# Talking-heads attention with a squared-ReLU FFN: the last 64 keys of two chunks post-mixed together

## The chip, the cores and the metric

The kernel runs on one core of a Trainium2 chip. The metric is the device time of one execution in microseconds (us). Before the change it was 520.69 us, the median of three runs (520.1 to 522.92).

## The reference

Eight batches of 12-head attention, 448 queries and keys, head size 64, in which the heads are mixed twice: the scores by `w_pre` ahead of the softmax, the probabilities by `w_post` behind it. A two-layer FFN with a squared ReLU follows.

```python
scores = scale * np.matmul(q, k.transpose(0, 1, 3, 2))           # (8, 12, 448, 448)
scores = np.einsum('bhij,hg->bgij', scores, w_pre)
attn = np.exp(scores - np.max(scores, axis=-1, keepdims=True))
attn = attn / (np.sum(attn, axis=-1, keepdims=True) + 1e-09)
attn = np.einsum('bhij,hg->bgij', attn, w_post)
x = np.matmul(attn, v)                          # to (8 * 448, 12 * 64) rows
h = np.maximum(x @ w_in, 0.0)                   # w_in (768, 2048)
return (h * h) @ w_out                          # w_out (2048, 768)
```

## The kernel before

Every engine's instructions are written out by a planner. `ORDER` is a string of digits, each naming a stream of TensorE units (0 transposes of q and k, 1 QK, 2 pre-mix, 3 post-mix, 4 attention times v, 5 direct chunks of batch 0, 6 and 7 the first FFN layer, 8 and 9 the second); TensorE runs the units in this order. The other engines' work is placed by the planner when its inputs are due, by the costs in the code; a copy out of PSUM marked `FLEX` goes to ScalarE (ACT) or VectorE (DVE). GpSimd (POOL) folds and issues the loads and most stores in one queue, SyncE (SP) issues the moves from `stage` to `dring`.

*Attention.* A unit of QK gives 128 (or 64) queries of a head pair; its scores go through `stage`, and a DMA brings them to `dring`, where a chunk of 10 queries has its 12 heads on the partitions. The pre-mix is a matmul over these 120 rows. ACT takes the exponential into the ring `pring` (12 chunks) and sums each row (`rowsum`). DVE takes the reciprocal (`rinv`), and POOL (DVE for the first chunks) folds it into the post-mix weights: `wk2s` = `wk2b` x `rinv`, for a pair of chunks at a time.

*Post-mix* (`emit_post`). The exponentials are the stationary operand, 128 keys at a time, `wk2s` (60 columns) the moving one. A chunk's two halves of 5 queries stand on partitions 0 to 59 and 64 to 123, and run as two row tiles side by side. 448 keys are three and a half slots of 128: there are four slots (`NS`, `KEYS`), and two of them share 64 keys, so that a pair of chunks takes 16 matmuls. The result goes by two evictions of 480 columns to `a2t`, keys on partitions, one `a2t` for each half of a batch (220 and 228 queries).

*Attention times v* (`emit_AV`), once for each half batch, a "part". `vraw` holds the keys of v in the same four slots. In a part, 40 matmuls over 128 keys stand in 128x64 tiles (heads on two column tiles), and 8 matmuls over 64 keys in 64x64 tiles (`fn_half`, ahead of the others) serve the slots that are used by half; for the last heads a zeroed half of `vraw` is multiplied along. Three evictions, one for each pair of head pairs, bring the result to `xt`, the FFN's input.

*FFN.* From batch 2 on it runs in row tiles or 64x64 tiles, in two phases, so that a second phase waits for the first. Tile shapes on TensorE in the order's rows: QK with 128 rows, post-mix, L1278 and L1413 are row tiles; pre-mix, transposes, L1292 and L1427 are 64x64; L1211 is 128x64; L1257 and L1362 use the whole array.

## Time and profile before

| | |
|---|---|
| median of 3 runs | 520.69 us |
| the profiled execution: its span | 520.6 us |
| TensorE busy | 505.5 us (97%), 10859 matmuls |
| ACT busy | 425.6 us (82%) |
| DVE busy | 398.7 us (77%) |
| POOL busy | 203.4 us (39%) |
| TensorE's clock | full in all 40 slices |

The span reaches from the first to the last instruction of the profiled execution, which is all of its own time that the page has. Busy shares are means over stages: the kernel starts with direct matmuls for batch 0 and ends with the FFN of batch 7 alone. In the profile a line number is that of the program; most copies have the one line of a helper (L526 on ACT, L527 on DVE), so the tile's name tells them apart. PEld is the load of a stationary operand, which overlaps the matmuls.

### The profile page before, as it was taken

The page shows a single profiled execution, that of the slowest core. Times are in us where ns is not written, and L with a number is a line of the kernel's source. Part 1 is how long each engine was busy: PE and PEld are TensorE (multiplying, and loading weights), DVE is VectorE, ACT ScalarE, POOL GpSimd, SP SyncE. Part 2 cuts the span into 40 slices and gives each one's busy share as a digit, 9 for nine tenths or more (in the row PEclk, how much of TensorE's full clock was granted, in tenths as well). Part 3 has the DMA queues.
Part 4 walks back from the last instruction along what each step waited for, and adds up shares of the span by engine and source line. Part 5 has one row for each costly group of instructions (what it writes and reads, how often), then busy time and mean ns, then how long its engine had stood idle before and what let it go on. Part 6 is the DMA issues. An engine that isn't in the chain of part 4 may idle for free.

```text
span 520.6 us, 25670 instructions
## 1 busy us (share of the span) xinstructions
PE 505.5 (97%) x10859; PEld 340.1 (65%) x10859; DVE 398.7 (77%) x1004; ACT 425.6 (82%) x1206; POOL 203.4 (39%) x404
## 2 busy tenths in 40 slices
PE   8999999899999999999999999999999999999996
PEld 4555777668766665667657665667666666678963
DVE  6967988789987869967997779976887669757430
ACT  4799999879998898989887999988788879878311
POOL 9914364325632384134622464225440333123010
PEclk9999999999999999999999999999999999999999
DMA  8999999646893699347974689457972568432013
GB/s 160 208 218 184 197 194 184 156 107 144 167 180 86 136 177 197 92 112 166 178 156 90 153 175 179 98 111 170 167 151 59 125 140 148 91 81 69 4 39 90
DMA packets 82724, 72.12 MB, mean 139 GB/s; under 512 B 13578, under 2 KB 80090, under 8 KB 82602
## 3 DMA queue, kind: packets, MB, share of 16 engines
q0 software_dynamic: 36944, 32.81, 38.5%
q1 hardware_dynamic: 45370, 37.38, 29.7%
q8 instruction: 89, 1.46, 1.1%
q14 instruction: 33, 0.27, 0.1%
q10 hardware_dynamic: 288, 0.20, 0.1%
HBM read 45.70 MB, written 11.01 MB: 109 GB/s over the span
## 4 chain that ended last, share of the span: by engine, by line
PE 92%; DMA 3%; DVE 2%; issue 2%; ACT 1%; POOL 0%; DVEq 0%
PE ps L1413 17%; PE ps L1278 12%; PE ps L1427 9%; PE ps L1292 9%; PE ps L1133 8%; PE ps L1052 8%; PE ps L1257 6%; PE ps L1211 6%; PE ps L922 5%; PE ps L974 4%; DMA dring<-stage 3%; PE ps L825 2%; PE ps L1362 2%; PE ps L986 2%; PE ps L649 1%
## 5 line engine op out<-in xcount | busy, mean ns | idle before, releaser
L1070 ACT ACTIVATE pring<-ps 128x448 bf16<-128x448 f32 x360 | 192.0, 550 | 12.6 <-PE ps L1052 7.3
L1101 POOL TENSOR_TENSOR wk2s<-wk2b,rinv 128x120 bf16<-128x120 bf16 (+1 forms) x179 | 69.0, 389 | 223.5 <-DVE rinv L1094 222.8
L527 DVE CAST a2t<-ps 128x480 bf16<-128x480 f32 (+1 forms) x201 | 122.1, 640 | 18.4 <-PE ps L1133 16.9
L527 DVE CAST stage<-ps 128x448 bf16<-128x448 f32 (+1 forms) x189 | 112.8, 618 | 19.0 <-PE ps L986 8.7
L526 ACT ACTIVATE stage<-ps 128x448 bf16<-128x448 f32 (+1 forms) x171 | 87.9, 549 | 18.2 <-PE ps L986 10.6
L526 ACT ACTIVATE a2t<-ps 128x480 bf16<-128x480 f32 x167 | 88.2, 570 | 15.5 <-PE ps L1133 15.0
L1413 PE MATMUL ps<-w_out_sb,h2t 64*128 64x384 bf16 x1056 | 95.9, 322 | 0.0
L1070 ACT ACTIVATION_READ_ACCUMULATOR pring<-ps 128x1 f32 x360 | 76.9, 214 | 0.0
L1133 PEld LDWEIGHTS ps<-wk2s,pring 60*128 60x128 bf16 x2880 | 54.9, 93 | 24.7 <-issue 5.8
L1278 PE MATMUL ps<-xt,w_in_sb 64*128 64x448 bf16 (+2 forms) x840 | 70.6, 309 | 0.0
L1413 PEld LDWEIGHTS ps<-w_out_sb,h2t 64*128 64x128 bf16 x1056 | 48.4, 94 | 31.1 <-PE ps L1052 0.7
L1459 POOL DMA_DIRECT2D out_dram<-osb x59 | 36.9, 632 | 75.9 <-DVE osb L527 25.8
L1133 PE MATMUL ps<-wk2s,pring 60*128 60x60 bf16 x2880 | 62.3, 187 | 1.9 <-issue 1.4
L1052 PE MATMUL ps<-dring,wk 64*64 64x448 bf16 (+1 forms) x676 | 61.5, 359 | 2.4 <-issue 1.2
L1427 PE MATMUL ps<-w_out_sb,h2t 64*64 64x384 bf16 x1216 | 57.4, 323 | 0.9 <-issue 0.8
L1323 DVE TENSOR_SCALAR h1t<-ps 128x448 bf16<-128x448 f32 (+2 forms) x96 | 46.2, 488 | 12.6 <-PE ps L1278 9.1
L1292 PE MATMUL ps<-xt,w_in_sb 64*64 64x448 bf16 (+1 forms) x1008 | 54.5, 345 | 0.8 <-issue 0.6
L1332 DVE TENSOR_TENSOR h2t<-h1t 128x448 bf16<-128x448 bf16 (+2 forms) x176 | 52.0, 331 | 1.4 <-ACT h1t L1322 0.9
L1322 ACT ACTIVATE h1t<-ps 128x448 bf16<-128x448 f32 (+2 forms) x80 | 35.4, 448 | 19.7 <-PE ps L1278 13.9
L1094 DVE RECIPROCAL rinv<-rowsum 128x2 f32<-128x2 f32 (+1 forms) x184 | 29.3, 160 | 28.2 <-ACT pring L1070 27.1
L1278 PEld LDWEIGHTS ps<-xt,w_in_sb 64*128 64x128 bf16 x840 | 38.3, 94 | 18.1 <-DVE rinv L1094 0.5
L1427 PEld LDWEIGHTS ps<-w_out_sb,h2t 64*64 64x64 bf16 x1216 | 38.2, 107 | 13.8 <-issue 2.0
(70 smaller groups left out, 595.0 us busy)
## 6 DMA issues: line engine op xcount, KB each, us to landing
dring<-stage SPq DMA_DIRECT2D x309, 105.0 KB
out_dram<-osb POOLq DMA_DIRECT2D x45, 192.0 KB, 3.7
qraw<-in_q_dram POOLq DMA_DIRECT2D x42, 112.0 KB, 5.3
kraw<-in_k_dram POOLq DMA_DIRECT2D x42, 112.0 KB, 6.2
w_in_sb<-in_moe_w_in_dram POOLq DMA_DIRECT2D x8, 384.0 KB, 16.3
w_out_sb<-in_moe_w_out_dram POOLq DMA_DIRECT2D x8, 384.0 KB, 11.9
vraw<-in_v_dram POOLq DMA_DIRECT2D x21, 128.0 KB, 4.8
vraw<-in_v_dram POOLq DMA_DIRECT2D x21, 96.0 KB, 5.0
```

The lines of the kernel that those rows point to most:

```text
L526: return eng.activation(o, i_, AF.Copy)
L527: return eng.tensor_copy(o, i_)
L1052: r_ = eng.matmul(ps[64 * y:64 * y + 64, gr.banks[x], 0:S], wk1[64 * x:64 * x + 64 - R0 * x, :], dring[64 * x:64 * x + 64 - R0 * x, (g0 + ...
L1070: return eng.activation(pring[:, pr, 0:S], ps[:, gr.banks[x], 0:S], AF.Exp, accum_out=rowsum[:, rs, :])
L1101: return eng.tensor_tensor(wk2s[:, p0:p0 + n, :], i0.to_broadcast([128, n, PR]), rinv[:, p0:p0 + n, :].to_broadcast([128, n, PR]), ALU.mult)
L1133: r_ = eng.matmul(ps[:, gr.banks[x], o0:o0 + PR], pring[64 * x:64 * x + PR, pr + y, j0:j0 + 2 * PJ], wk2s[64 * x:64 * x + PR, pr + y, :], ...
L1278: r_ = eng.matmul(ps[:, g.banks[x], 0:n], w_in_sb[64 * y:64 * y + 64, ft, t * 128:(t + 1) * 128], xt[64 * y:64 * y + 64, ft, c0:c1], start ...
L1292: r_ = eng.matmul(ps[64 * z:64 * z + 64, g.banks[x], 0:n], w_in_sb[64 * y:64 * y + 64, ft, t:t + 64], xt[64 * y:64 * y + 64, ft, c0:c1], s ...
L1323: return eng.tensor_scalar(h1t[:, box[0], 0:n], ps[:, g.banks[x], 0:n], 0.0, None, op0=ALU.max)
L1332: return eng.tensor_tensor(h2t[:, t16, o0:o0 + n], h1t[:, box[0], 0:n], h1t[:, box[0], 0:n], ALU.mult)
L1413: r_ = eng.matmul(ps[:, g.banks[hh], 0:FH], h2t[64 * y:64 * y + 64, t16, col:col + 128], w_out_sb[64 * y:64 * y + 64, t16, hh * FH:(hh + 1 ...
L1427: r_ = eng.matmul(ps[64 * z:64 * z + 64, g.banks[hh], 0:FH], h2t[64 * y:64 * y + 64, t16, col + 64 * z:col + 64 * z + 64], w_out_sb[64 * y ...
```

## The change

The keys are cut into three whole slots of 128 and a rest of 64 (`NS` = 3, `NM` = 7 blocks of `a2t` in place of 8).

*Fold.* `pring` gets 60 more columns behind the 448 exponentials, with a copy of `wk2b` (`wk2c`, once, on ACT), and the fold multiplies the last 128 columns of each chunk (64 exponentials and the 60 weights with 4 zeros) by `rinv`: 256 elements for a pair, not 120.

*Post-mix.* The three whole slots go as before, 12 matmuls for a pair. The rest of both chunks goes in one matmul on each row tile: the scaled exponentials of both are the stationary operand (64 + 64 columns), the unscaled `wk2b` the moving one. The first chunk's rest then stands on partitions 0 to 63, the second's on 64 to 127. A pair takes 14 matmuls and two evictions of 420 columns; the single last chunk of a batch takes 8, as before.

*Attention times v.* 36 matmuls over 128 keys come first, 12 for each of three banks. The rest follows in three phases of 8 matmuls in 64x64 tiles (`avq..._0` to `_2`), each with 110 or 118 columns. Each waits for the phase before it, and the banks are complete after the second phase (one) and the third (two). `a2t` now holds one member's queries of each pair behind the other's, so each `xt` eviction is two copies of 220 columns with a permuted target, and a third one of 16 columns in a second half.

*Loads, constants, order.* `vraw` has six slots, all loads of v bring four of them (128 KB), and q and k of batches 2 to 7 may load ten chunks earlier. The planner's constants and the string `ORDER` are new.

```diff
-MODE_SWITCH = 106.0
+MODE_SWITCH = 100.0
-FETCH = (2450.0, 0.3, 2400.0, 0.3, 600.0)
+FETCH = (3560.0, 0.3, 2400.0, 0.3, 600.0)
 ORDER = (
-    "0001501510105151555555555555555551335510015555555553335510021551355553255310055511255321"
...
+    "0010150011055115555555555555515555555550033551115555501105553335352555535131500555211555"
...
-    NS = 4
-    POS = (0, 3, 5, 1, 4, 6, 2)
-    KEYS = (0, 3 * PJ, 5 * PJ, PJ)
+    NS = 3
+    NM = 2 * NS + 1
+    POS = (0, 2, 4, 6, 1, 3, 5)
+    KT = NS * 2 * PJ
...
+        def fn_wk2c(eng, en):
+            i_ = wk2b[:, :, :].rearrange("p a b -> p (a b)").unsqueeze(1).to_broadcast(
+                [128, NPS, PR])
+            return eng.activation(pring[:, :, S:S + PR], i_, AF.Copy)
...
-            s0, n = (0, NS) if (h0 == 4) == (u == 1) else (u, NS - 1)
+            n = NS + 1
...
-                            after = [chain["t"], pre_at((b - 1) * NCP + 2 + 2 * n)]
+                            after = [chain["t"], pre_at((b - 1) * NCP - 8 + 2 * n)]
...
             def fn_fold(eng, en):
-                i0 = wk2b[:, :, :].rearrange("p a b -> p (a b)").unsqueeze(1)
                 return eng.tensor_tensor(
-                    wk2s[:, p0:p0 + n, :], i0.to_broadcast([128, n, PR]),
-                    rinv[:, p0:p0 + n, :].to_broadcast([128, n, PR]), ALU.mult)
+                    wk2s[:, p0 // 2, :, 0:n, :].rearrange("p k y e -> p y k e"),
+                    pring[:, p0:p0 + n, KT:].rearrange("p y (k e) -> p y k e", k=2),
+                    rinv[:, p0:p0 + n, :].unsqueeze(2).to_broadcast([128, n, 2, PJ]), ALU.mult)
...
                 for y in range(n):
                     for s in range(NS):
-                        o0 = (y * NS + s) * PR
+                        o0 = (n * s + y) * PR
                         for x in range(2):
                             r_ = eng.matmul(
                                 ps[:, gr.banks[x], o0:o0 + PR],
-                                pring[64 * x:64 * x + PR, pr + y, j0:j0 + 2 * PJ],
-                                wk2s[64 * x:64 * x + PR, pr + y, :],
+                                pring[64 * x:64 * x + PR, pr + y, 2 * PJ * s:2 * PJ * (s + 1)],
+                                wk2s[64 * x:64 * x + PR, pr // 2, 1, y, 0:PR],
                                 start=True, stop=True,
                             )
+                o0 = n * NS * PR
+                for x in range(2):
+                    r_ = eng.matmul(
+                        ps[:, gr.banks[x], o0:o0 + PR],
+                        wk2s[64 * x:64 * x + PR, pr // 2, 0, :, :].rearrange("p y e -> p (y e)"),
+                        wk2b[64 * x:64 * x + PR, :, :].rearrange("p a b -> p (a b)"),
+                        start=True, stop=True,
+                    )
...
+            done_at = ((), (1,), (0, 2))
...
+            for ph in range(NP // 2):
+                use = (ph, (ph + 1) % (NP // 2))
+
+                def fn_rest(eng, en, ph=ph, use=use):
+                    r_ = None
+                    for x in range(2):
+                        for z, kk in QUADS:
+                            bank = use[z]
+                            h = 2 * (2 * bank + x) + kk
+                            o0 = (2 * x + z) * al
+                            w = AL[0] if z else al
+                            r_ = eng.matmul(
+                                ps[kk * 64:kk * 64 + 64, gs[bank].banks[0], o0:o0 + w],
+                                vraw[64 * z:64 * z + 64, h, 0 if z else NS + 1, :],
+                                a2t[half][64 * z:64 * z + 64, h, 2 * NS, 0:w],
+                                start=False, stop=(x == 1 and bank in done_at[ph]),
+                            )
+                    return r_
+
+                was = t_av
+                t_av = unit(s_AV, "avq%d_%d_%d" % (b, c0, ph), fn_rest, [was],
+                            2 * (al / 2.4 + 6.0), "quad", None, 8)
+                t_av.sync = [was]
...
                 def fn_x(eng, en, p=p, g=g):
...
+                    for a in range(2):
+                        d = xt[:, p + a, c0:c0 + n].rearrange(
+                            "p (m c t) -> p m c t", c=2, t=CH // x_)
+                        r_ = copy(eng, en, d, src[:, a, :, 0:AL[0]].rearrange(
+                            "p c (m t) -> p m c t", t=CH // x_))
+                    if al > AL[0]:
+                        r_ = copy(eng, en, xt[:, p:p + 2, c0 + n:c1], src[:, :, 0, AL[0]:al])
```

Where the order moves TensorE, two places. The rows are TensorE's instructions in order: line, result and operands, shape of the result, how many alike. First, the attention times v of the first half of batch 6 before the change (L825 transposes, L1292 first FFN layer, L974 QK, L1052 pre-mix, L1427 second FFN layer):

```order
L1292 MATMUL ps<-xt,w_in_sb 64x448 x24
L1190 MATMUL ps<-a2t0,vraw 64x220 x8
L974 MATMUL ps<-qkt 64x448 x4
L1211 MATMUL ps<-a2t0,vraw 64x220 x40
L1052 MATMUL ps<-dring,wk1 64x448 x8
L1427 MATMUL ps<-w_out_sb,h2t 64x384 x32
```

and after it (L836 transposes, L985 QK, L1063 pre-mix, L1469 second FFN layer, L1209 and L1235 attention times v):

```order
L985 MATMUL ps<-qkt 64x448 x4
L1209 MATMUL ps<-a2t0,vraw 64x220 x36
L1235 MATMUL ps<-a2t0,vraw 64x110 x8
L1063 MATMUL ps<-dring,wk1 64x448 x4
L1235 MATMUL ps<-a2t0,vraw 64x110 x8
L1469 MATMUL ps<-w_out_sb,h2t 64x384 x32
L1235 MATMUL ps<-a2t0,vraw 64x110 x8
```

The 64x64 matmuls moved from ahead of the 128x64 ones to behind them, in three pieces with another unit between two of them. Elsewhere a post-mix unit, in row tiles, stands between.

Second, the way from the second half of batch 3 to the first FFN layer, before (L1133 post-mix):

```order
L1211 MATMUL ps<-a2t1,vraw 64x228 x40
L974 MATMUL ps<-qkt 128x448 x2
L1133 MATMUL ps<-wk2s,pring 128x60 x16
L1052 MATMUL ps<-dring,wk1 64x448 x4
L1292 MATMUL ps<-xt,w_in_sb 64x448 x24
```

and after, from the end of the third phase (L1320 first FFN layer, L1144 and L1152 post-mix):

```order
L1235 MATMUL ps<-a2t1,vraw 64x118
L1235 MATMUL ps<-a2t1,vraw 64x110
L1063 MATMUL ps<-dring,wk1 64x448 x4
L985 MATMUL ps<-qkt 128x448 x2
L1320 MATMUL ps<-xt,w_in_sb 128x448 x12
L1144 MATMUL ps<-wk2s,pring 128x60 x12
L1152 MATMUL ps<-wk2b,wk2s 128x60 x2
```

Between the last matmul over v and the first of the FFN stood three units, now two; post-mix units follow behind.

More of the change, by code (lines that the diff above doesn't have):

```diff
@@ L462, in bass_talking_heads_attention__then__ffn_squared_relu_kernel @@
         wall = early[:, 512:512 + NP * 2 * H].rearrange("p (n x h) -> p n x h", n=NP, x=2)
-        pring = sb("pring", [128, NPS, S], DT.bfloat16)
-        a2t = [sb("a2t%d" % i, [128, NS, H, HC[i] * CH], DT.bfloat16) for i in range(2)]
+        pring = sb("pring", [128, NPS, 512], DT.bfloat16)
+        AL = (HC[0] * H5, HC[0] * H5 + TAIL)
+        a2t = [sb("a2t%d" % i, [128, H, NM, AL[i]], DT.bfloat16) for i in range(2)]
         xt = sb("xt", [128, NP, S], DT.bfloat16)
@@ L1224, in fn_x @@
-                def fn_x(eng, en, p=p, g=g, x_=x_):
-                    return copy(eng, en, xt[:, p:p + 2, c0:c1],
-                                ps[:, g.banks[x_], 0:2 * n].rearrange("p (x n) -> p x n", x=2))
+                                    ps[kk * 64:kk * 64 + 64, g.banks[0],
+                                       2 * x * al:2 * (x + 1) * al],
+                                    vraw[:, h, s + 1, :],
+                                    a2t[half][:, h, 2 * s:2 * s + 2, :],
+                                    start=(x == 0 and s == 0), stop=False,
+                                )
@@ new lines, in fn_av @@
+                    return r_
+                avs.append(unit(s_AV, "av%d_%d_%d" % (b, c0, p), fn_av,
+                                a2 + v_of[b] + ([t_zero[0]] if half else []),
+                                2 * NS * (2 * al / 2.4 + 2.9), "cols", g, 4 * NS))
+            t_av = None
+            done = {}
+            for ph in range(NP // 2):
[19 more added lines that the diff above has]
+                t_av.sync = [was]
+                t_av.after += [avs[i] for i in use]
+                for i in done_at[ph]:
+                    done[i] = t_av
@@ new lines, in emit_AV, with fn_x @@
+            for p in range(0, NP, 2):
+                g = gs[p // 2]
+                def fn_x(eng, en, p=p, g=g):
+                    n = 2 * AL[0]
+                    x_ = 1 if b * NCP + c0 < ND else 2
+                    src = ps[:, g.banks[0], 0:4 * al].rearrange(
+                        "p (a c n) -> p a c n", a=2, c=2)
+                    for a in range(2):
[5 more added lines that the diff above has]
+                        r_ = copy(eng, en, xt[:, p:p + 2, c0 + n:c1], src[:, :, 0, AL[0]:al])
+                    return r_
+                more = 200.0 if half else 70.0
@@ L1486, in bass_talking_heads_attention__then__ffn_squared_relu_kernel @@
                 t_wk2 = add("wk2", DVE, fn_wk2, [t_wsmall, t_mask2], {DVE: (300.0, 400.0)}, -450.0)
+                t_wk2c = add("wk2c", ACT, fn_wk2c, [t_wk2], {ACT: (820.0, 930.0)}, -2e6)
                 emit_load_qk(1)
```

130 lines of the change are left out of this document (54 added, 76 removed).

## The prediction

> **What bounds the kernel now.** I read the page first, then the busy time by stage, then TensorE's timeline at an attention-times-v part, then groups by shape and the waits. The page gives the shares and the chain that ended last:
>
> ```profile
> span 520.6 us, 25670 instructions
> PE 505.5 (97%) x10859; PEld 340.1 (65%) x10859; DVE 398.7 (77%) x1004; ACT 425.6 (82%) x1206; POOL 203.4 (39%) x404
> PE 92%; DMA 3%; DVE 2%; issue 2%; ACT 1%; POOL 0%; DVEq 0%
> ```
>
> TensorE carries 92% of the chain; ACT and DVE have a fifth to spare, GpSimd (POOL) more than half. The busy times by stage say where TensorE still stands still:
>
> ```profile
> 48.00:100.00 52.00, 48.14 (x1010) 36.30 (x1010) 44.64 (x127) 47.70 (x141) 23.08 (x47) 1.00 0.99 187
> 100.00:200.00 100.00, 98.49 (x2178) 69.69 (x2180) 83.84 (x212) 90.30 (x265) 46.27 (x93) 1.00 0.72 145
> 484.00:521.00 37.00, 31.57 (x428) 22.93 (x416) 8.88 (x32) 7.85 (x18) 2.52 (x4) 0.98 0.18 47
> ```
>
> From 48 to 100 us it lacks 3.9 us, from 100 to 200 us 1.5 us, and the last stage lacks 5.4 us, most of it behind the last matmul (last evictions and output). The profiled execution's span is 520.6 us, 0.1 us under the median of the runs (520.69), so I sum against 520.6.
>
> A saturated stretch of TensorE's timeline gives its prices (start, length, work, count; a unit's price is start to start, as matmuls overlap):
>
> ```profile
> 250.90 0.39 PE L1133 MATMUL ps<-wk2s,pring 60*128 60x60 bf16 x16
> 251.12 0.35 PE L974 MATMUL ps<-qkt 64*128 64x448 bf16 x2
> ...
> 253.81 0.54 PE L974 MATMUL ps<-qkt 64*128 64x448 bf16 x4
> 254.28 0.38 PE L1052 MATMUL ps<-dring,wk 64*64 64x448 bf16 x4
> 254.49 1.31 PE L1292 MATMUL ps<-xt,w_in_sb 64*64 64x448 bf16 x24
> 255.63 0.36 PE L1052 MATMUL ps<-dring,wk 64*64 64x448 bf16 x4
> 255.82 1.31 PE L1292 MATMUL ps<-xt,w_in_sb 64*64 64x448 bf16 x24
> ```
>
> A post-mix unit of 16 matmuls takes 0.22 us, 13.75 ns each. Four 64x448 matmuls in 64x64 tiles take 0.19 us, and 24 take 1.14 us (254.49 to 255.63): 47.5 ns each, 0.106 ns a column. A change of tile shape has a price of its own: the four row-tiled QK matmuls at 253.81 need 2 x 0.19 = 0.38 us, but the next unit, in 64x64 tiles, starts 0.47 us later. So 0.09 us, and 0.1 us with the other direction in mind.
>
> **The change, part by part.**
>
> *Post-mix.* A pair of chunks takes 14 matmuls for 16; the single last chunk of a batch keeps 8. 8 batches x 22 pairs x 2 x 13.75 ns = 4.8 us less on TensorE, all on the path.
>
> *Attention times v.* One part's matmuls and the way to the next layer, before:
>
> ```profile
> 243.54 2.16 PE L1211 MATMUL ps<-a2t,vraw 128*64 128x228 bf16 x40
> 245.63 0.36 PE L974 MATMUL ps<-qkt 64*128 64x448 bf16 x2
> 245.83 0.39 PE L1133 MATMUL ps<-wk2s,pring 60*128 60x60 bf16 x16
> 246.15 0.38 PE L1052 MATMUL ps<-dring,wk 64*64 64x448 bf16 x4
> 246.36 1.31 PE L1292 MATMUL ps<-xt,w_in_sb 64*64 64x448 bf16 x24
> ```
>
> 40 matmuls of 228 columns take 2.09 us with one change of shape behind them: 1.99 us, 0.218 ns a column. A second half had 40 x 228 of these and 8 x 228 in 64x64 tiles (1.99 + 0.19 = 2.18 us); it gets 36 x 236 and 12 x (118 + 110) (1.85 + 0.29 = 2.14). A first half goes from 40 x 220 and 8 x 220 (1.92 + 0.19 = 2.11) to 36 x 220 and 24 x 110 (1.73 + 0.28 = 2.01). Over eight of each 0.14 x 8 = 1.1 us; small matmuls never run quite at the rate of wide ones, so I take 0.9 us. Work on TensorE: -5.7 us.
>
> *Changes of tile shape.* The rest's three 64x64 phases must not run into each other, so each waits for the one ahead, and the order puts other units between. Counted over TensorE's whole order, the shape changes 224 times before and 255 times now. 31 x 0.1 = +3.1 us, all on the path. Here more than half of the saved work is given back.
>
> *Waits of TensorE on itself.* 32 new ones (second and third phase of 16 parts). In 29 a unit stands between, in 3 (batch 0) nothing. The nearest rows are a second phase of the first FFN layer behind one short unit:
>
> ```profile
> 258.93 1.46 PE L1292 MATMUL ps<-xt,w_in_sb 64*64 64x448 bf16 x24
> 260.07 0.51 PE L974 MATMUL ps<-qkt 64*64 64x448 bf16 x4
> 260.45 0.76 PE L1292 MATMUL ps<-xt,w_in_sb 64*64 64x448 bf16 x12
> ```
>
> Here the second phase starts 0.38 us behind the short unit, not 0.19: a wait of 0.19 us, with 448 columns draining. That is the upper end for a covered wait of 110 columns, 29 x 0.19 = 5.5 us; the lower end is nothing, as where a post-mix or pre-mix unit covers it elsewhere. The bare ones cost at most 0.39 us, the length of a post-mix unit's drain (250.90). I take 3 x 0.2 + 29 x 0.01 = +0.9 us, since 110 columns drain sooner than 448.
>
> *Evictions.* An `a2t` eviction falls from 480 to 420 columns; the groups by shape price a column:
>
> ```profile
> L527 DVE CAST a2t<-ps 128x480 bf16<-128x480 f32 x193 | 119.6, 651 | 16.6 <-PE ps L1133 15.2
> L526 ACT ACTIVATE a2t<-ps 128x480 bf16<-128x480 f32 x159 | 86.1, 582 | 13.4 <-PE ps L1133 12.8
> L527 DVE CAST a2t<-ps 128x192 bf16<-128x192 f32 x8 | 2.8, 354 | 1.7 <-PE ps L1133 1.7
> L526 ACT ACTIVATE a2t<-ps 128x192 bf16<-128x192 f32 x8 | 2.7, 339 | 2.1 <-PE ps L1133 2.1
> L1101 POOL TENSOR_TENSOR wk2s<-wk2b,rinv 128x120 bf16<-128x120 bf16 x171 | 66.8, 393 | 219.9 <-DVE rinv L1094 219.2
> L1101 POOL TENSOR_TENSOR wk2s<-wk2b,rinv 128x60 bf16<-128x60 bf16 x8 | 2.3, 290 | 3.7 <-DVE rinv L1094 3.6
> L1322 ACT ACTIVATE h1t<-ps 128x220 bf16<-128x220 f32 x22 | 7.7, 364 | 3.0 <-PE ps L1278 2.1 <-PE ps L1292 0.5
> L526 ACT ACTIVATE xt<-ps 128x456 bf16<-128x456 f32 x13 | 7.2, 554 | 1.3 <-PE ps L1211 1.0
> ```
>
> DVE: (651 - 354) / 288 = 1.03 ns a column, ACT 0.84. 193 x 62 ns + 159 x 51 ns = 20 us less on the two together. The `xt` evictions go the other way: one copy of 440 or 456 columns (0.55 us) becomes two of 220 (0.36 us each), and a second half adds one of 16. 48 x 0.2 to 0.4 us = +10 to +19 us. Both lie beside TensorE, and nearly cancel. The copy of the folded weights into the ring (`wk2c`, 720 columns, once on ACT) is near 0.06 + 720 x 0.84 ns = 0.7 us, ahead of the first exponentials, while TensorE works off the direct matmuls; without that cover it would cost its 0.7 us.
>
> *From the last phase to the first FFN layer.* In the fence of 243.54 this way is 245.63 to 246.36, 0.73 us, with only the last of three evictions left in it. Now two evictions hang on the third phase, each with two or three copies, and in the second halves of batches 2, 3 and 4 the order leaves only a pre-mix and one other unit between (0.19 + 0.2 + 0.1 = 0.49 us). One engine needs 0.36 + 0.25 + 0.2 = 0.8 us and hand-overs; so 0.3 to 0.75 us each, 0.9 to 2.3 us in all. I take +0.9 us, since the two run on two engines.
>
> *The fold on GpSimd.* 256 elements instead of 120. (393 - 290) / 60 = 1.72 ns each, so 393 + 136 x 1.72 = 627 ns, +0.23 us on 171 folds (40 us on an engine that has 317 us free). It delays a post-mix by 0.23 us where the order leaves no room. The waits before:
>
> ```profile
> PE ps L825 <- issue: 1.8, 2, 1.0
> PE ps L1133 <- issue: 1.4, 3, 0.6
> PE ps L1052 <- issue: 1.2, 2, 1.0
> PE ps L1427 <- issue: 0.8, 2, 0.6
> PE ps L1292 <- issue: 0.6, 1, 0.6
> PEld ps L1133 <- POOL wk2s L1101: 1.4, 3, 0.7
> ```
>
> TensorE's post-mix waited three times for a fold. I put the fold at 0 to +6 us (0: six pairs are in the ring; 6: 26 of the 184 come late by its full 0.23), and take 0 because three waits are much nearer to none than to 26. Loads: half of the V loads grow from 96 to 128 KB, 0.8 MB of 72 MB; q and k loads of batches 2 to 7 are let go five pairs earlier. Both lie beside work.
>
> *Stalls that a new order can move.* "issue" above is TensorE out of instructions: 1.8 + 1.4 + 1.2 + 0.8 + 0.6 = 5.8 us at ten places. The start-to-start prices over all 10859 matmuls come to 467 us and 224 changes of shape to 22; of the other 31 us about half lies at the start and the end, so some 15 us are stalls of the body, these 5.8 among them. The new order and lighter evictions can take from it up to 6 us; they can add up to 5 us, since several evictions now have less distance to their user. I take -2.2 us, two fifths of the 5.8: there are 12 back-to-back pairs of transpose units where there were 16, and those use up instructions fastest. This is the weakest term.
>
> **Sum.** -5.7 + 3.1 + 0.9 + 0.9 + 0 - 2.2 = -3.0 us: 520.6 - 3.0 = 517.6 us. A difference under 0.5%, 2.6 us, could not be told from none.
>
> **The rivals.**
>
> *The order gives it all back* (no change). The stalls stay as they are: -0.8 us, 519.8 us. For it: 31 more shape changes and three tight ends of parts. Against it: 20 us less to evict.
>
> *Post-mix waits for GpSimd* (slower). Folds stand in POOL's one queue behind DMA issues of some 0.6 us, and one that is late holds TensorE, with the chunk's evictions and everything queued behind it. At 0.23 us a fold and full stalls it takes 26 late folds (+6 us) to turn -0.8 into 525.8 us; from about 15 on the change is slower than before. Three waits in the trace speak against that many, but the trace has no fold of this size.
>
> *DVE blocked by the longer folds.* A fold and DVE's squares both read two SBUF tensors; if one blocks the other, longer folds slow the squares, and the second FFN layer waits for those.
>
> ```profile
> L1332 DVE TENSOR_TENSOR h2t<-h1t x176: 253/279/578, 56.3 to 499.2; 128x448 bf16<-128x448 bf16 x80, 128x220 bf16<-128x220 bf16 x48, 128x228 bf16<-128x228 bf16 x48
> ```
>
> Folds occupy 13% of the span now and would occupy 21%; 176 squares x (0.21 x 0.31 - 0.13 x 0.2) us = 7 us more on DVE. If a third of it reached TensorE, 520 us; if all, 524.6. [...]
>
> *More is gained* (faster still). Waits fall by 6 us, not 2.2: 513.8 us.
>
> **How the numbers follow.** 517.6 us has 0.38, the greater gain 0.10, no change 0.32, the late folds 0.14, the blocked squares 0.06 (half of it slower than before by over 0.5%). Faster by over 0.5% is the first two, 0.48. Slower is the late folds and half of the last, 0.17; the same is 0.35. The range runs from 513 us, the greater gain with a little of the unsure `xt` term, to 523.5 us, where half of the late folds' price has come; it leaves out the far half of each outer case. The likeliest case alone spans 515 to 519 us.
>
> **What would show it.** After: the post-mix 0.19 us a pair; `a2t` evictions near 590 and 530 ns; a fold near 627 ns; TensorE's waits on itself in the new 64x64 phases under 1 us in all; "issue" under 4 us; and in batches 2, 3 and 4 a gap of a few tenths ahead of the first FFN matmul. The prediction is wrong if post-mix rows wait for `wk2s` in more than a dozen places, if small 64x64 phases take over 0.12 us each, or if the waits of the body do not fall.

## The result, and the profile after

| | median | runs | ratio to before |
|---|---|---|---|
| before | 520.39 us | 516.68 to 522.92 | |
| after | 538.81 us | 537.27 to 540.43 | 1.0344 (95%: 1.0288 to 1.0399) |

The change made the kernel 18 us slower; 517.6 us was predicted. Executions more than 1.5% above the fastest of their kernel are left out of the medians and ranges below: one each of `before_oa` and `shortfold`, two of `al_nostage`. The page of the changed kernel, with the lines that answer to those of before (span, busy time, SyncE's queue of moves, the chain that ended last):

```profile
span 538.7 us, 25472 instructions
PE 510.8 (95%) x10723; PEld 332.6 (62%) x10723; DVE 404.3 (75%) x1048; ACT 429.8 (80%) x1236; POOL 243.0 (45%) x404
q1 hardware_dynamic: 45370, 37.38, 31.2%
PE 74%; DMA 9%; ACT 9%; DVE 3%; POOL 1%; issue 1%; SPq 0%; DVEq 0%; ACTq 0%
```

The trace has 136 matmul records fewer, yet TensorE is busy 5 us longer and idle 28 us in place of 15. Its share of the chain falls from 92% to 74%, and DMA's rises from 3% to 9%. The busy times by stage (stretch, its length, TensorE, its weight loads, DVE, ACT, POOL, clock, DMA share, GB/s), first before, then after, show where:

```profile
200.00:300.00 100.00, 98.54 (x2300) 64.20 (x2298) 83.22 (x189) 88.68 (x250) 38.34 (x78) 1.00 0.66 141
300.00:400.00 100.00, 98.92 (x2356) 65.07 (x2354) 81.31 (x190) 88.74 (x250) 40.21 (x81) 1.00 0.71 140
```

```profile
48.00:100.00 52.00, 49.99 (x978) 35.28 (x976) 46.32 (x130) 48.62 (x152) 29.08 (x47) 1.00 1.01 185
100.00:200.00 100.00, 95.77 (x2014) 66.72 (x2012) 82.62 (x219) 87.85 (x261) 56.67 (x95) 1.00 0.75 146
200.00:300.00 100.00, 93.17 (x2140) 58.64 (x2138) 79.87 (x189) 85.04 (x240) 39.40 (x64) 1.00 0.67 129
300.00:400.00 100.00, 94.34 (x2069) 58.59 (x2066) 76.48 (x188) 83.36 (x242) 51.86 (x86) 0.98 0.78 149
```

TensorE lacks 4.2, 6.8 and 5.7 us in the three full stages, where it lacked 1.5, 1.5 and 1.1 us. ACT and DVE are less busy there too, so no engine of the body is at its limit. What they wait for is new. Waits of the `stage` evictions for moves, before, then after with TensorE's two longest (who, for what: us, times, longest):

```profile
DVE stage L527 <- DMA dring<-stage: 0.9, 1, 0.9
```

```profile
DVE stage L532 <- DMA dring<-stage: 17.9, 8, 4.1
ACT stage L531 <- DMA dring<-stage: 11.7, 5, 3.6
PE ps L836 <- DVE h1t L1365: 2.8, 1, 2.8
PE ps L1209 <- ACT stage L531: 2.7, 1, 2.7
```

ACT and DVE stand 29.6 us before an eviction to `stage` that may not start until SyncE's moves have read that slot of it (two slots; 0.9 us on DVE before the change). One such place, in ACT's, DVE's and TensorE's timelines:

```profile
249.73 0.25 ACT L1081 ACTIVATION_READ_ACCUMULATOR pring<-ps 128x1 f32 x1
253.34 0.54 ACT L531 ACTIVATE stage<-ps 128x448 bf16<-128x448 f32 x1 [3.35 <-DMA dring<-stage]
253.78 1.09 ACT L531 ACTIVATE xt<-ps 128x220 bf16<-128x220 f32 x4
```

```profile
248.87 0.36 DVE L532 CAST a2t<-ps 128x192 bf16<-128x192 f32 x1
253.34 0.62 DVE L532 CAST stage<-ps 128x448 bf16<-128x448 f32 x1 [4.11 <-DMA dring<-stage]
```

```profile
250.47 0.81 PE L1209 MATMUL ps<-a2t,vraw 128*64 128x236 bf16 x12
253.93 1.48 PE L1209 MATMUL ps<-a2t,vraw 128*64 128x236 bf16 x24 [2.66 <-ACT stage L531]
```

Both engines take their work in a fixed order. From 249.2 us on DVE and 250.0 us on ACT each has a `stage` eviction at the head of its queue, the last move lets both go at 253.34, and meanwhile PSUM banks stay full and TensorE stops. The moves themselves have become slower. SyncE's issue of a move (ns: shortest, median, longest), before and after:

```profile
L1029 SPq DMA_DIRECT2D dring<-stage x367: 664/799/2333, 16.2 to 466.7; - x184
```

```profile
L1040 SPq DMA_DIRECT2D dring<-stage x367: 664/902/2735, 16.3 to 481.5; - x184
```

The number and bytes of the moves are the same, and so are the lines that issue them; the diff changes only the planner's price for an issue, from 1050 to 900 ns.

Behind the longest of TensorE's waits the granted clock falls as well. The 2.8 us for `h1t` end at 394.56 us; from 396.1 us on the clock is half for 3.4 us (columns as in the table by stage; the clock is the third number from the right):

```profile
390.00:395.00 5.00, 2.20 (x75) 1.22 (x66) 2.27 (x5) 2.29 (x6) 0.00 (x0) 1.00 0.51 98
395.00:400.00 5.00, 4.94 (x95) 2.79 (x88) 3.48 (x11) 3.65 (x14) 2.92 (x5) 0.66 0.69 126
```

By estimate that is 1.7 us of work not done, and it counts as busy time. The mean granted clock was 0.991 to 0.996 in the four executions after the change.

### The profile page after: what moved, and what is told of

It is laid out like the page before. It is cut to its first block, busy times and chain, and to the rows that moved or that the text cites. A ratio compares the mean times of both kernels' runs of the same rounds, so it can differ in the third digit from the quotient of the medians.

```text
span 538.7 us, 25472 instructions
## 1 busy us (share of the span) xinstructions
PE 510.8 (95%) x10723; PEld 332.6 (62%) x10723; DVE 404.3 (75%) x1048; ACT 429.8 (80%) x1236; POOL 243.0 (45%) x404
## 4 chain that ended last, share of the span: by engine, by line
PE 74%; DMA 9%; ACT 9%; DVE 3%; POOL 1%; issue 1%; SPq 0%; DVEq 0%; ACTq 0%
PE ps L1455 14%; PE ps L1320 11%; DMA dring<-stage 8%; PE ps L1469 8%; PE ps L1334 7%; PE ps L1063 6%; PE ps L1299 5%; PE ps L1144 5%; PE ps L933 5%; ACT pring L1081 4%; PE ps L1209 4%; PE ps L985 3%; ACT stage L531 3%; PE ps L1404 2%; PE ps L836 2%
## 5 line engine op out<-in xcount | busy, mean ns | idle before, releaser
L1081 ACT ACTIVATE pring<-ps 128x448 bf16<-128x448 f32 x360 | 192.3, 556 | 19.4 <-PE ps L1063 14.3
L1111 POOL TENSOR_TENSOR wk2s<-pring,rinv 128x256 bf16<-128x256 bf16 (+1 forms) x179 | 109.1, 617 | 217.3 <-DVE rinv L1105 216.7
L532 DVE CAST a2t<-ps 128x420 bf16<-128x420 f32 (+1 forms) x204 | 122.1, 640 | 9.9 <-PE ps L1152 8.4
L531 ACT ACTIVATE a2t<-ps 128x420 bf16<-128x420 f32 (+1 forms) x164 | 96.3, 654 | 12.5 <-PE ps L1152 12.1
L1320 PE MATMUL ps<-xt,w_in_sb 64*128 64x448 bf16 (+2 forms) x840 | 77.4, 322 | 2.3 <-issue 1.5
L1081 ACT ACTIVATION_READ_ACCUMULATOR pring<-ps 128x1 f32 x360 | 79.3, 220 | 0.0
L1063 PE MATMUL ps<-dring,wk 60*64 60x448 bf16 (+1 forms) x676 | 60.1, 361 | 3.9 <-DVE osb L532 1.5
L1144 PEld LDWEIGHTS ps<-wk2s,pring 60*128 60x128 bf16 x2160 | 45.3, 93 | 26.5 <-ACT pring L1081 3.2
L1469 PE MATMUL ps<-w_out_sb,h2t 64*64 64x384 bf16 x1280 | 59.7, 323 | 0.3 <-issue 0.2
L1374 DVE TENSOR_TENSOR h2t<-h1t 128x448 bf16<-128x448 bf16 (+2 forms) x176 | 57.3, 353 | 1.3 <-ACT h1t L1364 0.5
L1144 PE MATMUL ps<-wk2s,pring 60*128 60x60 bf16 x2160 | 53.4, 188 | 3.9 <-DVE stage L532 1.3
L1320 PEld LDWEIGHTS ps<-xt,w_in_sb 64*128 64x128 bf16 x840 | 37.7, 94 | 27.7 <-issue 3.2
L1334 PE MATMUL ps<-xt,w_in_sb 64*64 64x448 bf16 (+2 forms) x1008 | 48.3, 330 | 0.1
L1469 PEld LDWEIGHTS ps<-w_out_sb,h2t 64*64 64x64 bf16 x1280 | 39.7, 107 | 12.3 <-issue 0.6
```

The lines of the kernel that those rows point to most:

```text
L531: return eng.activation(o, i_, AF.Copy)
L532: return eng.tensor_copy(o, i_)
L1063: r_ = eng.matmul(ps[64 * y:64 * y + 64, gr.banks[x], 0:S], wk1[64 * x:64 * x + 64 - R0 * x, :], dring[64 * x:64 * x + 64 - R0 * x, (g0 + ...
L1081: return eng.activation(pring[:, pr, 0:S], ps[:, gr.banks[x], 0:S], AF.Exp, accum_out=rowsum[:, rs, :])
L1111: return eng.tensor_tensor(wk2s[:, p0 // 2, :, 0:n, :].rearrange("p k y e -> p y k e"), pring[:, p0:p0 + n, KT:].rearrange("p y (k e) -> p ...
L1144: r_ = eng.matmul(ps[:, gr.banks[x], o0:o0 + PR], pring[64 * x:64 * x + PR, pr + y, 2 * PJ * s:2 * PJ * (s + 1)], wk2s[64 * x:64 * x + PR, ...
```

## The experiments

Each is told with its edit, what was expected on record, and what came out; the times of before beside them were 519.4 to 520.6 us.

### Evictions in longer runs

`runs35`: `a2t` with the 7 key slots beside each other. The padding tile ahead of the weights goes from 128 to 64 bytes with it, which matters further below.

```diff
-        a2t = [sb("a2t%d" % i, [128, H, NM, AL[i]], DT.bfloat16) for i in range(2)]
+        a2t = [sb("a2t%d" % i, [128, H, PX[i], NM, H5], DT.bfloat16) for i in range(2)]
...
-                    d = a2t[half][:, :, 0:NM:3 - n, at + x * nt:at + (x + 1) * nt]
+                    d = a2t[half][:, :, px + x, 0:NM:3 - n, 0:nt]
...
-        sb("align", [128, 128], DT.uint8)
+        sb("align", [128, 64], DT.uint8)
```

> The changed kernel with a2t laid out as [head, query piece, 7 key slots, 5 queries], so that each eviction writes runs of 35 elements instead of runs of 5, and the xt evictions of all but the first part copy straight columns; order, loads and the planner's costs are the changed kernel's. Theory B (runs of 5 make the a2t evictions dear, and ScalarE and VectorE fall behind): ScalarE's a2t eviction falls from 669 to about 520 ns, VectorE's from 653 to about 590, together over 30 us less on the two, and the time falls by 10 to 17 us, to 522-529. Theory A (the moves of the scores come late, and the stage evictions hold both engines until they end, whatever these have to do): evictions get shorter, the waits on dring<-stage stay near 30 us in sum, and the time is 534-539. A loss is possible too: the attention matmuls now read their moving operand in runs of 10; each 10 ns on one of the 576 would cost 5.8 us, seen at the attention line.

`flat`: every eviction writes one straight run, and attention reads straight.

```diff
-                    d = a2t[half][:, :, 0:NM:3 - n, at + x * nt:at + (x + 1) * nt]
+                    w_ = H * m * nt
+                    f0 = (c0 - half * HC[0]) * H * NM * H5 + x * w_
+                    d = a2t[half][:, :, :, :].rearrange("p h m i -> p (h m i)")[
+                        :, f0:f0 + w_].rearrange("p (h m t) -> p h m t", h=H, m=m)
```

> The changed kernel, every a2t eviction writing its 420 columns as one straight run, so that attention reads its operand straight too (as it does in the changed kernel); what is left out is that each weight reaches its own key and query. It has the cheaper evictions of the run with runs of 35 (541 and 587 ns) without that run's dearer attention matmuls (295 instead of 266 ns). Theory B with a share of the loss: 528-534, 5 to 10 us below the changed kernel. Theory A alone: 535-539.

`before5`: the kernel before with runs of 5 everywhere.

```diff
-                    if g0 < ND:
+                    if True:
...
-                            :, :, :, x * H5:(x + 1) * H5]
+                            :, :, :, x * (nt // n):(x + 1) * (nt // n)]
```

> The kernel before, with every a2t eviction writing runs of 5 (the form that it uses for the direct chunks of its first batch) instead of 10; the order of query columns within a pair is then another, so output rows are exchanged. Theory B says ScalarE's a2t eviction goes from 582 to about 680 ns and VectorE's from 651 to about 658; if the scattered write alone made the loss, the time would be 530 or more. Theory A, or ScalarE's slack before (73% busy) taking it up: 520-525.

The groups of `a2t` evictions by shape, in the changed kernel, in `flat`, and in `before5`:

```profile
L531 ACT ACTIVATE a2t<-ps 128x420 bf16<-128x420 f32 x156 | 94.4, 669 | 11.0 <-PE ps L1152 10.6
L532 DVE CAST a2t<-ps 128x420 bf16<-128x420 f32 x196 | 119.9, 653 | 9.9 <-PE ps L1152 8.4
```

```profile
L531 ACT ACTIVATE a2t<-ps 128x420 bf16<-128x420 f32 x156 | 75.5, 527 | 15.4 <-PE ps L1153 14.7
L532 DVE CAST a2t<-ps 128x420 bf16<-128x420 f32 x196 | 109.1, 587 | 11.6 <-PE ps L1153 9.9
```

```profile
L526 ACT ACTIVATE a2t<-ps 128x480 bf16<-128x480 f32 x159 | 102.3, 705 | 10.7 <-PE ps L1133 10.2
L527 DVE CAST a2t<-ps 128x480 bf16<-128x480 f32 x193 | 125.9, 691 | 15.2 <-PE ps L1133 13.7
```

Runs of 5 are dear, as theory B has it. But `flat` took 538.3 us (537.1 to 540.1) with 30 us less on the two engines, and `before5` 521.2 us (1.0021, 0.9984 to 1.0058) with 22 us more (its page of before has ACT busy for 82%, not the 73% of the expectation). So the price lies beside TensorE, and theory B falls as a cause of the loss. `runs35` gave 540.3 us: cheaper evictions again (541 and 587 ns), but its attention matmuls read in runs of 10 and became dearer, from 259 to 276 and from 266 to 295 ns each.

### Stage evictions that need not wait

`nostage`: the moves read another tile.

```diff
-                              stage[r0:r0 + nv, n % 2, :, :]).then_inc(sem.handle, 16)
+                              qkt[r0:r0 + nv, b % 2, :, :, :].rearrange(
+                                  "p a i s -> p (a i) s")).then_inc(sem.handle, 16)
...
+            if t.name.startswith("sev"):
+                t.deps = [d for d in t.deps if not d.name.startswith("rel")]
```

> The changed kernel whose moves read queries and keys (qkt) in place of stage, so that no stage eviction has to wait for a move; instruction order, sizes and numbers of the moves are the same; what is left out is that the scores themselves reach the pre-mix. Theory A (stage evictions that wait for moves block ScalarE and VectorE): their waits on dring<-stage go to zero, TensorE's stalls of 1 to 3 us near 205, 250, 314 and 390 us go, and the time falls by 10 to 18 us, to 521-529. Theory B or D (too much work on the two engines, or the order itself): 533-539. If the moves themselves are what is late, TensorE waits for them at the pre-mix instead, and the time stays over 530.

`flat_nostage`: this edit and that of `flat`.

> The run before this one, with moves that read queries and keys in place of stage as well, so that no stage eviction waits for a move (left out: the scores reaching the pre-mix, and the places of the weights). If A and B together make the loss, the time comes to that of the kernel before or below it: 515-523. If something else holds as much as 5 us (order, loads, fold): 525-530.

530.7 us (527.5 to 531.1) and 529.7 us (527.7 to 532.8). The wait alone is worth 8 us of the 18, a little less than theory A had, and the cheaper evictions on top of it 1 us, which the spread of the runs covers. The third case of the expectation, TensorE waiting at the pre-mix in place of the evictions, has the time on its side (just over 530) but not the trace, in which TensorE waits for no move. The two edits together did not reach the time before, so something else holds as much again; and why the moves were late was open.

### What could make the moves late

`after_cb`: the planner's constants of the kernel before for DMA, code fetch and changes of tile shape, and its two functions for the DMAs.

```diff
-MODE_SWITCH = 100.0
+MODE_SWITCH = 106.0
-FETCH = (3560.0, 0.3, 2400.0, 0.3, 600.0)
+FETCH = (2450.0, 0.3, 2400.0, 0.3, 600.0)
...
-DMA_AHEAD = 1250.0
+DMA_AHEAD = 3900.0
...
-                rate = (0.312, 0.67) if b[2] <= 200.0 else (0.15, 0.48)
+                rate = (0.22, 0.52)
```

> The changed kernel with the planner's constants for DMA, code fetch and tile-shape change of the kernel before; TensorE's order is the same, the order on ScalarE, VectorE, GpSimd and SyncE and the choice between ScalarE and VectorE for each eviction may differ. Theory F (the new constants expect moves too early, so evictions stand in the queues ahead of others that could run): 522-532. Theories A, B and D without it: within 3 us of 538.8.

536.8 us (532.9 to 539.0). The waits for moves fell from 29.6 to 9.1 us (7.7 on DVE, 1.4 on ACT), the time by 2: where the queues were laid out so that evictions wait less, TensorE waited at other places. So the sum of these waits is no measure of the loss by itself. Theory F holds a tenth at most, and the moves' issue stays at 901 ns.

`shortfold` (128 elements a fold) and `before_fold2` (each fold twice):

```diff
-                    wk2s[:, p0 // 2, :, 0:n, :].rearrange("p k y e -> p y k e"),
-                    pring[:, p0:p0 + n, KT:].rearrange("p y (k e) -> p y k e", k=2),
-                    rinv[:, p0:p0 + n, :].unsqueeze(2).to_broadcast([128, n, 2, PJ]), ALU.mult)
+                    wk2s[:, p0 // 2, 1, 0:n, :],
+                    pring[:, p0:p0 + n, S:],
+                    rinv[:, p0:p0 + n, :].to_broadcast([128, n, PJ]), ALU.mult)
...
-                        wk2s[64 * x:64 * x + PR, pr // 2, 0, :, :].rearrange("p y e -> p (y e)"),
+                        pring[64 * x:64 * x + PR, pr, KT - PJ:S],
```

> The changed kernel whose fold scales only the weights (128 elements a pair, as in the kernel before, instead of 256); the post-mix of the rest takes 128 unscaled exponentials as its stationary operand, so what is left out is the rest's scaling and half of its data; the number, shapes and order of matmuls are the same. Theory C (the longer fold is at the root: GpSimd's 626 ns take something from SyncE's moves, whose issue went from a median of 799 to 902 ns, and from VectorE): fold near 380 ns, move issue back to about 800 ns, waits on dring<-stage under 8 us instead of 29.6, time 522-531. If the fold is harmless: move issue stays at 900 ns, time 536-541.

```diff
+            if g >= 10:
+                t_fold = add("fold2%d_%d" % (b, c), POOL, fn_fold, [t_fold],
+                             {POOL: (10.0, 10.0)}, b * 1000.0 - 900 + c)
```

> The kernel before with each fold on GpSimd done twice (the second waits for the first, and the post-mix for the second), about 0.76 us a pair on GpSimd and 0.45 us later. Theory C: move issue rises from 799 to 880 ns or more, waits on dring<-stage appear, time 527-538. If GpSimd's work is harmless: 519-524, with some waits of the post-mix for wk2s.

539.2 us (538.2 to 542.6) with folds of 411 ns, the moves' issue stays at 912 ns and the waits on `dring<-stage` at 25.9 us; 522.6 us (1.0046, 1.0012 to 1.0079), issue 819 ns and 5.4 us of such waits. GpSimd is not the cause of the slow moves.

`after_loads` and `v96`:

```diff
-                            after = [chain["t"], pre_at((b - 1) * NCP - 8 + 2 * n)]
+                            after = [chain["t"], pre_at((b - 1) * NCP + 2 + 2 * n)]
```

> The changed kernel with the query and key loads let go at the chunks of the kernel before (ten chunks later). Theory E (earlier loads collide with the moves): move issue back to about 800 ns, waits on dring<-stage under 8 us, time 523-531. If not: 535-541, or worse where the loads now come late for the transposes.

```diff
-            n = NS + 1
+            n = NS + 1 if b == 0 else NS
+            s0 = 1 - u if b == 0 else 1
...
```

> The changed kernel whose value loads from the second batch on bring 3 of the 4 key slots (96 KB instead of 128 KB; left out: the rest's own values, those of the first batch stand in). Theory E in its other form (more bytes to load): move issue back towards 800 ns, waits on dring<-stage halved, time 525-533. If size does not matter: 536-541.

541.0 and 536.6 us, issue 916 and 926 ns. Neither the time of the loads nor their size makes the moves slow. In `after_loads` the waits on `dring<-stage` fell to 10.8 us and the time did not fall at all, as in `after_cb`; in `v96` they were 19.4 us, and its 2 us lie within the noise.

### The order of TensorE

`after_ob` has the digits of before, with each part's third and fourth 4 doubled; `before_oa` the digits of after, with the second and fourth of a part's six left out.

```diff
-    "0010150011055115555555555555515555555550033551115555501105553335352555535131500555211555"
...
+    "0001501510105151555555555555555551335510015555555553335510021551355553255310055511255321"
...
```

> The changed kernel's work in TensorE's order of the kernel before: the digit string of before, with the third and fourth turn of each part's attention doubled, since a part now has six units instead of four. Theory D (the new order itself brings more shape changes and worse places): 520-530. Otherwise 534-542, or worse, since that string was made for other durations.

```diff
-    "0001501510105151555555555555555551335510015555555553335510021551355553255310055511255321"
...
+    "0010150011055115555555555555515555555550033551115555501105553335352555535131500555211555"
...
```

> The kernel before with its work in TensorE's order of the changed kernel (two of the six attention turns of a part left out of the digit string). Theory D: 530-540, with stage evictions that wait for moves as in the changed kernel. If the new order does harm only together with the changed evictions and loads: 520-526.

557.0 and 537.4 us. Both lose, so they tell little on which order is the better one: a string made for one kernel suits the other badly. `before_oa` changes tile shape 296 times in place of 224 in the records of its timeline, some 7 of its 17 us by the prediction's 0.1 us; `after_ob` changes it 254 times, as the changed kernel does (255), and loses 18 us more all the same. In the trace of `before_oa` (548.4 us) `stage` evictions wait 9.9 us for moves, as theory D expected, though the moves are issued in 806 ns. So the places in the order can bring such waits without slow moves; the up to 10 us that they hold could not be parted from the misfit.

### Where the tiles begin

Every form of the changed kernel had issued its moves in 887 to 935 ns, every form of before in 797 to 819. What the forms share is the memory map. `wk2s` grew from 12 x 60 x 2 = 1440 bytes to 6 x 2 x 2 x 64 x 2 = 3072. If the tiles lie one behind the other as the program names them, which the author assumed (no view shows addresses), `w_in_sb` and the large tiles behind it, `stage` and `dring` among them, moved by 1632 bytes a partition, 12 x 128 + 96; those behind `vraw` and `pring` moved by another 12 x 128 for each. So all of these stand 96 bytes off their old places, mod 128. Behind the first `a2t` (18480 bytes, no multiple of 128 now) `xt`, `h1t` and `h2t` stand off by another distance, in `after_al` too. The expectations below speak of starts on multiples of 128 and 64; that the tiles of before stood on multiples of 128 is an assumption as well, and the runs show distances from their places alone. The kernel has a tile for nothing but padding ahead of them, and three runs change its size alone. `after_al`:

```diff
-        sb("align", [128, 128], DT.uint8)
+        sb("align", [128, 32], DT.uint8)
```

> The changed kernel with the padding tile ahead of the weights cut from 128 to 32 bytes a partition, so that all the large tiles begin on a multiple of 128 bytes as in the kernel before, in place of 32 bytes off a multiple of 64; not one instruction changes. Theory H (tiles that begin off a multiple of 64 make the moves and some of VectorE's work slower): move issue back to about 800 ns, the squares of 448 columns back from 415 to about 396 ns, waits on dring<-stage under 5 us, time 515-526. If the start address does not matter: 537-541 with the same durations.

`after_al64`, and `before_mis` with the same line in the kernel before:

```diff
-        sb("align", [128, 128], DT.uint8)
+        sb("align", [128, 96], DT.uint8)
```

> The kernel before with the padding tile cut from 128 to 96 bytes, so that its large tiles begin 32 bytes off a multiple of 64. Theory H: move issue rises from 799 to about 900 ns, the squares from 396 to about 415 ns, waits on dring<-stage appear, time 526-538. If the start address does not matter: 518-522.

> The changed kernel with the padding tile cut to 96 bytes, so that the large tiles up to the first a2t begin on odd multiples of 64 bytes. If a multiple of 64 is enough, as after_al: 515-526; if 128 is needed, it stays near 538; half way, if moves need the one and engines the other.

| | bytes off the place in before, mod 128, of the large tiles up to the first `a2t` | median | ratio to before |
|---|---|---|---|
| `after_al` | 0 | 528.6 us (526.7 to 531.8) | 1.0174 (1.0136 to 1.0212) |
| `after_al64` | 64 | 537.8 us (534.7 to 539.3) | 1.0342 (1.0305 to 1.0380) |
| after | 96 | 538.8 us | 1.0344 |
| `before_mis` | 96 | 524.4 us (521.2 to 527.2) | 1.0087 (1.0054 to 1.0121) |

SyncE's issue of a move in `after_al`, in `after_al64` and in `before_mis`:

```profile
L1040 SPq DMA_DIRECT2D dring<-stage x367: 664/799/2510, 16.3 to 466.3; - x184
```

```profile
L1040 SPq DMA_DIRECT2D dring<-stage x367: 665/901/2942, 16.4 to 474.4; - x184
```

```profile
L1029 SPq DMA_DIRECT2D dring<-stage x367: 665/907/2303, 16.2 to 467.4; - x184
```

The median is 799 ns in both kernels where the tiles stand in their old places, mod 128, and 902 to 907 where they stand 96 off. In `after_al64`, 64 off, it is 901 ns and nothing is won. (`runs35` stands 32 off: 935 ns. The shifts by whole 128s here are even multiples, 12 and more; an odd one was not run.) With nothing but 96 bytes of padding less, the waits and TensorE's busy time in `after_al` become:

```profile
DVE stage L532 <- DMA dring<-stage: 5.0, 4, 2.2
ACT stage L531 <- DMA dring<-stage: 3.4, 2, 2.1
```

```profile
200.00:300.00 100.00, 97.39 (x2186) 61.15 (x2184) 82.78 (x197) 88.75 (x253) 46.05 (x76) 1.00 0.66 135
300.00:400.00 100.00, 96.15 (x2214) 60.86 (x2213) 79.97 (x198) 87.40 (x253) 47.54 (x78) 1.00 0.71 142
```

8.4 us of waits in place of 29.6, and 9 to 10 of the 18 us are back (9.2 against `after_al64`, which ran beside it, 10.2 against after). The mean granted clock is 0.998 to 1.000 in the six executions, and the trace has no stretch at half clock, so by estimate 1.7 us of the gain lie there. The same 96 bytes cost the kernel before only 5 us: its `stage` evictions then wait 3.6 us on DVE. So the tiles' places make the moves slow. They do not do so by way of the engines' own instructions: after and `after_al` have the same means (on ACT 669 ns for an `a2t` eviction and 556 and 555 for an exponential, on DVE 616 for a `stage` eviction). That the cost depends on how close behind the moves the `stage` evictions stand is likely, as the two kernels differ so much, but no run shows it alone. One part of theory H fell: the squares stay at 415 ns in `after_al`.

### What holds the rest

Three runs put `after_al`'s edit together with that of `nostage`, of `flat` and of `after_cb`.

> The aligned form with moves that read queries and keys in place of stage, so that no eviction waits for a move (left out: the scores reaching the pre-mix). If the stage waits that are left (8.4 us in sum) still cost: 523-526. If the alignment had taken that loss away whole: 527-530. Either way this says whether the two runs without each, 530.7 and 528.6, took away the same microseconds or different ones.

> The aligned form of the changed kernel with a2t evictions that write one straight run (left out: each weight reaching its own key and query). If the rest of the loss is the work that the evictions of runs of 5 add to ScalarE and VectorE (some 30 us on the two): 520-525. If they lie beside TensorE, as they did without the alignment: 527-530.

> The aligned form with the planner's constants of the kernel before, which gave 2 us without the alignment and left 9.1 instead of 29.6 us of waits on dring<-stage. If the order of the evictions holds part of the rest: 523-527. If not: 527-531.

`al_nostage` took 525.0 us (1.0101, 1.0070 to 1.0132), `al_flat` 531.2 us (524.9 to 532.5), `al_cb` 533.9 us (531.0 to 538.3). Without the stage waits 3.7 us more are won, where 8 were won without the alignment; so about half of them were the same microseconds as those of the start addresses. The other way round, the alignment is worth some 6 us (530.7 to 525.0) where no eviction waits for a move, on a way that the runs leave open. Cheap evictions win nothing again. The constants of before, good for 2 us with slow moves, cost 5 with quick ones. Some 9 us against the kernel before stay in `after_al` and 5 in `al_nostage`, without one cause. No version here beats the kernel before.

## Why the prediction was wrong

*The step that failed* is the one that let alone what the diff does not name. "Loads: ... Both lie beside work" looked at the transfers whose issue changes; the moves were in no term, since the lines that issue them stay as they are. Their issue rose by 103 ns in the median, with the new places of the tiles, which follow from the new shape of `wk2s`. That put the term "stalls that a new order can move" on the wrong side: -2.2 us with bounds of -6 and +5. TensorE's idle time rose by 12.8 us, 27.9 in place of 15.1; the waits of the body did not fall, which the prediction had named as a sign of being wrong. The page of `after_al` says how much of that hangs on the start addresses:

```profile
span 524.9 us, 25472 instructions
PE 507.9 (97%) x10723; PEld 331.7 (63%) x10723; DVE 403.9 (77%) x1048; ACT 429.0 (82%) x1236; POOL 242.3 (46%) x404
```

17.0 us idle, so 10.9 of the 12.8 go with the start addresses (this execution took 526.7 us; by the medians it is 9 to 10 us of time). The range ended 15 us too low, and this is some two thirds of it.

The smaller part of the miss is on TensorE itself. Its work, shape changes and waits on itself were to come to -5.7 + 3.1 + 0.9 = -1.7 us of busy time; it rose by 5.3 us after (1.7 of them at half clock) and by 2.4 in `after_al`. Summed start to start over TensorE's timeline, idle time left out and a change of shape counted to the unit ahead of it, post-mix fell from 46.3 us to 41.3 in `after_al`, near the 4.8 predicted; attention times v rose from 36.9 to 39.8, pre-mix from 41.1 to 43.3, the first FFN layer from 150.4 to 152.6.

*TensorE's work.* Two post-mix units of 14, and a phase of 8 matmuls over 110 columns, with the unit behind each:

```profile
231.79 0.33 PE L1144 MATMUL ps<-wk2s,pring 60*128 60x60 bf16 x12
231.96 0.19 PE L1152 MATMUL ps<-wk2b,wk2s 60*128 60x60 bf16 x2
231.99 0.33 PE L1144 MATMUL ps<-wk2s,pring 60*128 60x60 bf16 x12
232.16 0.19 PE L1152 MATMUL ps<-wk2b,wk2s 60*128 60x60 bf16 x2
232.18 1.46 PE L1455 MATMUL ps<-w_out_sb,h2t 64*128 64x384 bf16 x16
...
249.46 0.29 PE L1235 MATMUL ps<-a2t,vraw 64*64 64x110 bf16 x8
249.58 0.36 PE L997 MATMUL ps<-qkt 64*64 64x448 bf16 x4
```

231.79 to 232.18 is 0.39 us for two, so 0.19 to 0.20 each, as predicted. The phase takes 0.12, which the prediction named as its limit; by its price of 0.106 ns a column it would be 0.09. So the small ones do run dearer here, 0.136 ns a column, as the prediction had it.

*Waits of TensorE on itself.* Mis-sized: +0.9 predicted. The bare ones at the two ends of batch 0 (start, length, count; next unit):

```profile
53.33 1.02 PE L1235 MATMUL ps<-a2t,vraw 64*64 64x110 bf16 x24
54.18 0.38 PE L1063 MATMUL ps<-dring,wk 64*64 64x448 bf16 x4
...
70.95 0.67 PE L1235 MATMUL ps<-a2t,vraw 64*64 64x118 bf16 x16
71.61 0.38 PE L1063 MATMUL ps<-dring,wk 64*64 64x448 bf16 x4
```

24 matmuls of 12 ns take 0.29 us and stand for 0.85; 16 take 0.2 and stand for 0.66. That is 1.0 us for three waits, where 0.6 was set. Of the covered ones, put at 0.01 us each, 14 wait 0.2 us, and they are in the waits of the weight loads:

```profile
PEld ps L1235 <- PE ps L1235: 2.6, 14, 0.2
```

So 2.6 to 3.6 us together, by whether these 14 hold the bare ones: 2 to 3 us more than was set, most of what attention times v rose by.

*Evictions.* "20 us less" was wrong: +0.3 us on DVE and +8.3 on ACT, as the rows of 119.9 and 94.4 us show. At equal runs of 5, 60 columns less save 36 ns on ACT and 38 on DVE (`before5` against after), where 51 and 62 were set; and the runs fell from 10 elements to 5, which costs more than that. That it costs no time was right: `flat` and `before5` moved 20 to 30 us of it without moving the time beyond its noise. The copy `wk2c` took 0.80 us where 0.7 was set (its 0.06 us agrees with the trace before: back to back, `stage` evictions of 448 columns start 0.42 us apart on ACT in the median, 0.05 more than 448 x 0.84 ns).

*Last phase to the first FFN layer.* The first FFN matmul waits for `xt` 0.4 us in all after and 0.6 in `after_al`; +0.9 was near enough. One engine's 0.25 us for a second copy of 220 columns holds too: in the trace after, the next instruction on ACT starts 0.23 us behind the start of such a copy in the median. "Issue" is 3.8 us, under the 4 predicted. That TensorE is out of instructions there agrees with the traces: nine of its ten such waits before, and six of seven after, end 2.2 to 2.5 us after a packet of 16 KB of the page's queue "q8 instruction" starts. Transposes do use them up fastest, 28 in 0.22 us (8 ns each, at 396.30 us before) beside 13.75 ns for a post-mix matmul.

*The fold.* 627 ns was predicted:

```profile
L1111 POOL TENSOR_TENSOR wk2s<-pring,rinv 128x256 bf16<-128x256 bf16 x171 | 106.1, 626 | 216.6 <-DVE rinv L1105 216.0
PEld ps L1144 <- POOL wk2s L1111: 2.1, 5, 0.7
```

Five waits, not a dozen, so the rival of late folds fell. The term of 0 may still be short: in `before_fold2` a whole second fold costs 0.6 to 4.1 us (1.0012 to 1.0079). The squares are slower, as the rival of the longer folds has it, but by little: 396 to 415 ns, 285 to 316 and 270 to 286, so 80 x 19 + 48 x 31 + 48 x 16 ns = 3.8 us on DVE, where the rival had 7. `shortfold` brings them back to 397 ns and `before_fold2` raises them to 422, so the fold does it; that one engine blocks the other no run shows, and what it costs in time was not parted.

*Changes of tile shape.* Both counts stand in the records (224 and 255), and a change still costs 0.1 us in them (four pre-mix matmuls at 229.99 us, row tiles 0.30 us later, not 0.19). As a sum, 31 x 0.1 us is not refuted and not shown: no run changed their number alone.

## What to carry to other kernels

A change of one small tile's size can move every tile behind it; here 96 bytes of padding less took the moves' issue from 902 to 799 ns and the time from 538.8 to 528.6 us. Compare the places of the tiles that DMAs read and write before and after, and keep them where they were, mod 128 bytes. When engines that were never the bound wait in long single pieces (3.4 and 4.1 us at 253 us here), look at what stands at the head of their queue, and then at the median of the transfer it waits for, also where the diff does not touch it. A cheaper or dearer eviction beside a full TensorE was worth nothing here, with the waits (`flat` 538.3 us beside 538.8, `before5` 521.2) and without them (`flat_nostage` 529.7 beside 530.7).

## What the runs showed of the hardware

*Start addresses.* Moves of rows of 896 bytes between SBUF tiles were issued in a median of 797 to 819 ns in the eight traces whose large tiles stand as in the kernel before, mod 128 bytes, in 887 to 935 ns in the twelve where they stand 32, 64 or 96 bytes off. The time of their packets, share of q1 by span, is 154.6 us of 16 engines before and 164.1 in `before_mis` (+6%), 156.9 in `after_al`, 162.5 in `after_al64` (+4%) and 168.1 after (+7%):

```profile
q1 hardware_dynamic: 45370, 37.38, 29.9%
```

```profile
q1 hardware_dynamic: 45370, 37.38, 31.6%
```

(`after_al`, then `before_mis`.) The issue takes as long 64 bytes off as 96 (901 and 902 ns), while the packets' time grows less (+4% and +7%). What in a start brings this about was not shown.

*Lengths of runs.* An eviction of 480 columns takes ACT 582 ns in runs of 10 bf16 elements and 705 in runs of 5, DVE 651 and 691. With 420 columns it is 669 (runs of 5), 541 (35) and 527 ns (straight) on ACT, and 653, 587 and 587 on DVE. The rows of before had a sign of it that the prediction passed over: its first batch writes runs of 5 already, and the 14 evictions of 480 columns on ACT in the first 62 us took 662 ns each, the 131 behind 100 us 574.

*Clock.* The 20 traces have 13 stretches of 3.4 us at half clock ahead of the last matmul. Each begins between 0.3 us before and 1.7 us after the end of a standstill of TensorE of 1.7 us or longer; 16 other standstills of that length had none. The trace of the kernel before has neither.
